# Two batches of a convolutional joint network: one batch through both convolutions first, joint tiles between the other's stages, pair sums chained in PSUM

## The chip, the cores and the metric

The kernel runs on one core of a Trainium2 chip. The metric is the device time in microseconds (us) of one execution. The engines are named as the profile names them: PE (TensorE matmul), PEld (TensorE weight load), DVE (VectorE), ACT (ScalarE), POOL (GpSimd), SP (SyncE, which issues most DMAs). PSUM is the memory that the matmuls write their sums to; the program divides it into eight banks. A stall is a stretch in which PE has nothing to run.

## The reference, cut to what matters

```python
B, T, D, K, U = 2, 4000, 512, 5, 8
def reference(x, w1, w2, g, w_f, w_g, w_o):
    h = sum over i<5 of  xp[:, i:i+T, :] @ w1[i]       # conv 1
    h = gelu(h)[:, ::2, :]                             # 2000 steps
    f = sum over i<5 of  hp[:, i:i+2000, :] @ w2[i]    # conv 2
    f = gelu(f)[:, ::2, :]                             # 1000 steps
    fe = f @ w_f ;  ge = g @ w_g
    j = tanh(fe[:, :, None, :] + ge[:, None, :, :])    # 1000 x 8 rows per batch
    return j @ w_o                                     # the joint product
```

Per batch there are two convolutions, one product "fe", and 1000 x 8 rows of the joint product. The kernel handles the joint product as 125 tiles of 128 rows, 62.5 for each batch. Each tile is four matmuls of 512 columns; the last is done in two halves, so that the profile counts 504 and not 500.

## The kernel before: the parts that matter

Both convolutions are computed with fast (Winograd-like) algorithms: sums and differences of inputs ("prepare") on DVE and ACT, sums of weights on DVE, fewer matmuls on PE. The first batch's conv 1 is done in three tiles (`Tile_`), everything else in `Triple`s with nine products per output chunk `m`.

A plan is made before the program is emitted. Every operation is recorded with what it reads and writes. A list scheduler then puts each engine's operations in order, from estimated costs. Afterwards each engine runs its list strictly in that order.

```python
def simulate(self, pred, succ, late):
    ...                                  # t, e: the engine that is free first, with something ready
        now = [i for i in cand[e] if ready[i] <= t + 0.02]
        i = min(now) if e in ("pe", "sp") else min(now, key=lambda i: (late[i], i))
    ...
```

PE takes the operation that comes first in program order among those that are ready; DVE and ACT take the most urgent by the scheduler's estimate. PSUM banks are handed out in program order, while the plan is recorded:

```python
banks = list(range(8))
def bank():                              # rotation, for fe and joint tiles
    banks.append(banks.pop(0))
    return banks[-1] * NT
```

A stage of a tile forms the pair sums with two DVE operations on two PSUM banks:

```python
def stages(self, m):                     # class Tile_
    n, lo = self.n, banks.pop(0)
    ...
    C, Dd = lo * NT, (lo + 1) * NT
    def sums():
        self.product("b2", m, C, True)
        self.product("a1", m, C, False)
        self.product("a2", m, Dd, True)
        c = cs[u % 2][0:n]
        act(c, ps.cols(C, n), ACT.Copy, scale=0.5)
        for o, f in ((C, 0.5), (Dd, -0.5)):
            stt("dve", ps.cols(o, n), ps.cols(Dd, n), f, c)
    def end0(): ...                      # a0, b1 accumulate onto C
    def end1(): ...                      # b3, a3 accumulate onto Dd, gelu
```

Prepare of conv 2 forms its differences by accumulating DMAs (issued on POOL):

```python
def prepare(self, by_dma=True):          # class Triple
    if by_dma:
        act(r32[1], z(0, 0, E), ACT.Copy, scale=-2.0)
        act(r32[2], z(2, 0, E), ACT.Copy, scale=-2.0)
        act(r32[0], z(4, -1, E), ACT.Copy, scale=-2.0)
        for i in (1, 2, 0):
            acc(r32[i], z(2 * i, 0, E))  # DMA with accumulate
    else:
        stt("dve", r32[1], z(0, 0, E), -2.0, z(2, 0, E))
        stt("dve", r32[2], z(2, 0, E), -2.0, z(4, 0, E))
        stt("dve", r32[0], z(4, -1, E), -2.0, z(0, 0, E))
    ...
```

And the order of the program is (`slot` puts the stages of one output chunk `m` into the program; the numbers after `m` in the later code say how many joint tiles follow each step): conv 1 of the first batch (three tiles), conv 1 of the second batch (`first[0]`, `first[1]`), conv 2 of the first (`trip[0]`), conv 2 of the second (`trip[1]`), then the joint tiles.

```python
for m in range(NK): slot(tiles[2], m) ...
for m in range(NK): slot(first[0], m) ...     # first[1].prepare, weight sums of conv 2 inside
for m in range(NK):
    slot(first[1], m)
    if m == 1:
        trip[0].prepare()
        load_last()
for m in range(NK): slot(trip[0], m) ...      # trip[1].prepare inside
for m in range(NK): slot(trip[1], m) ...      # ge, fe(0) inside
...
for jt in range(ntile): ...                   # 125 joint tiles; fe(1) at tile 8
```

## Time and profile before

| | before |
|---|---|
| time, median (four runs) | 270.9 us (270.75 to 271.46) |
| span in the profile | 269.3 us |
| PE / DVE / ACT busy | 261.0 / 198.2 / 181.7 us |
| PE idle between 20 and 120 us | 3.5 us |

These are lines of the profile page of the kernel before. The first two give busy time, share of the span and number of instructions of each engine. The others give the busy tenths of 40 equal slices of the span (6.7 us each), and the granted TensorE clock in tenths.

```profile
## 1 busy us (share of the span) xinstructions
PE 261.0 (97%) x1571; PEld 151.5 (56%) x1582; DVE 198.2 (74%) x288; ACT 181.7 (67%) x269; POOL 20.0 (7%) x32
...
PE   8999999999999988999999999999999999999995
...
DVE  0999999999999799697252365567666667656764
...
PEclk9999999999999999999999999999999999999999
```

PE is busy almost everywhere, at full clock. Apart from the first and the last slice, only two (94 to 108 us) fall below 9. DVE is full from about 7 to 83 us. So PE bounds the kernel, and the most that a reordering can win is PE's idle time.

The windows view gives that idle time in numbers. Its columns are the stretch and its length, then busy us and number of instructions of PE, PEld, DVE, ACT, POOL, then granted clock, DMA share and GB/s. Kernel before:

```profile
60.00:70.00 10.00, 9.51 (x63) 5.82 (x62) 10.00 (x13) 9.54 (x17) 2.92 (x3) 1.00 0.28 53
...
90.00:100.00 10.00, 8.69 (x61) 5.58 (x59) 8.01 (x14) 8.09 (x15) 1.32 (x2) 1.00 1.16 214
100.00:110.00 10.00, 9.30 (x66) 6.08 (x64) 9.93 (x13) 8.19 (x15) 2.73 (x3) 1.00 0.87 228
110.00:120.00 10.00, 9.51 (x68) 6.34 (x66) 7.86 (x12) 6.54 (x14) 1.28 (x1) 1.00 0.80 157
120.00:140.00 20.00, 20.00 (x156) 13.85 (x154) 10.71 (x18) 10.41 (x22) 0.00 (x0) 1.00 0.00 1
```

The missing parts of the ten-microsecond stretches from 20 to 120 us add up to 3.5 us (0.21 in 20 to 30, 0.49, 0.13, 0.18, 1.31, 0.70, 0.49 from 60 on). After 120 us PE has no stall worth naming.

What PE waited for in the worst stretch is in the timeline of PE, before. Its columns are start, length, engine, line, operation, output and inputs, count; in brackets, the idle time before it and what ended it.

```profile
96.45 0.74 PE L435 MATMUL acc<-zx,w_q 128*128 128x335 bf16 x4 [1.31 <-ACT sd L427]
102.59 0.74 PE L435 MATMUL acc<-hT,w_t 128*128 128x334 bf16 x4 [0.70 <-DVE hT L422]
```

### The profile page before, as it was taken

How to read it: one execution, taken by the hardware profiler on the slowest of the kernel's cores; microseconds unless marked ns; L12 is line 12 of the kernel's file. 1: busy time of each engine (PE TensorE's matmuls, PEld its weight loads, DVE VectorE, ACT ScalarE, POOL GpSimd, SP SyncE). 2: the span in 40 equal slices, each digit the busy share in tenths (PEclk: the TensorE clock that was granted, in tenths of full speed). 3: DMA queues.
4: the chain of work that ended last, by engine and by line, in shares of the span. 5: the costliest groups of instructions: out<-in, count | busy, mean ns of one | idle time of the engine just before them, and what ended most of it. 6: DMA issues, size and time to landing. Idle time of an engine off the chain costs nothing.

```text
span 269.3 us, 4218 instructions
## 1 busy us (share of the span) xinstructions
PE 261.0 (97%) x1571; PEld 151.5 (56%) x1582; DVE 198.2 (74%) x288; ACT 181.7 (67%) x269; POOL 20.0 (7%) x32
## 2 busy tenths in 40 slices
PE   8999999999999988999999999999999999999995
PEld 4897944466566645666766555444444444444442
DVE  0999999999999799697252365567666667656764
ACT  2667975459778697854489965579669769669110
POOL 1000000002533312300000000000000000000000
PEclk9999999999999999999999999999999999999999
DMA  7999999990996997940000130444544454443544
GB/s 247 306 176 223 168 177 197 197 333 4 179 215 121 212 207 234 223 87 2 0 1 2 39 117 22 153 147 136 165 161 155 133 164 149 163 155 126 170 151 142
DMA packets 61985, 40.13 MB, mean 149 GB/s; under 512 B 31742, under 2 KB 61710, under 8 KB 61966
## 3 DMA queue, kind: packets, MB, share of 16 engines
q1 hardware_dynamic: 54430, 31.49, 43.4%
q0 software_dynamic: 7392, 8.32, 16.9%
q8 instruction: 12, 0.20, 0.3%
q10 hardware_dynamic: 144, 0.07, 0.1%
q14 instruction: 7, 0.06, 0.1%
HBM read 7.86 MB, written 16.38 MB: 90 GB/s over the span
## 4 chain that ended last, share of the span: by engine, by line
PE 71%; DMA 12%; DVE 6%; issue 4%; SPq 2%; ACT 2%; POOL 2%; POOLq 0%; DVEq 0%
PE acc L435 71%; DMA r32b<-hT 6%; DMA half<-w_sb 2%; SPq L466 2%; DMA xs<-in_x_dram 2%; DMA w_sb<-in_w_dram 2%; POOL half L596 2%; DMA xr<-in_x_dram 1%; DVE hT L422 1%; DVE row L422 1%; DVE xt L422 1%; DVE row L756 1%; DVE w_t L422 1%; ACT hT L427 0%; DVE sd L422 0%
## 5 line engine op out<-in xcount | busy, mean ns | idle before, releaser
L435 PE MATMUL acc<-wo_sb,jT 128*128 128x512 bf16 (+1 forms) x493 | 107.5, 377 | 0.6
L1070 DVE CAST ost<-acc 128x512 bf16<-128x512 f32 (+1 forms) x105 | 72.2, 689 | 39.6 <-PE acc L435 39.6
L427 ACT ACTIVATE jT<-feT,geT 128x1000 bf16<-128x1000 f32 (+10 forms) x84 | 72.6, 927 | 16.9 <-PE acc L435 16.9
L435 PEld LDWEIGHTS acc<-wo_sb,jT 128*128 128x128 bf16 x504 | 49.3, 98 | 58.4
L427 ACT ACTIVATE ost<-acc 128x512 bf16<-128x512 f32 (+1 forms) x21 | 12.1, 577 | 22.5 <-PE acc L435 22.5
L435 PE MATMUL acc<-xt,w_sb 128*128 128x252 bf16 (+1 forms) x144 | 23.0, 305 | 0.2
L435 PE MATMUL acc<-row,w_sb 128*128 128x334 bf16 (+1 forms) x112 | 20.3, 305 | 0.0
L427 ACT ACTIVATE sd<-acc 128x334 f32<-128x334 f32 (+1 forms) x32 | 14.1, 447 | 8.6 <-PE acc L435 8.6
L435 PEld LDWEIGHTS acc<-xt,w_sb 128*128 128x128 bf16 x144 | 13.8, 98 | 7.5 <-DVE xt L422 1.0
L435 PE MATMUL acc<-row,w_t 128*128 128x334 bf16 (+1 forms) x80 | 14.6, 305 | 0.0
L435 PE MATMUL acc<-fT,wf_sb 128*128 128x333 bf16 (+1 forms) x96 | 14.0, 305 | 0.0
L435 PE MATMUL acc<-xs,w_t 128*128 128x252 bf16 (+1 forms) x76 | 13.9, 314 | 0.0
L427 ACT ACTIVATE hT<-acc 128x334 bf16<-128x334 f32 (+2 forms) x21 | 11.3, 552 | 3.8 <-PE acc L435 3.8
L435 PEld LDWEIGHTS acc<-row,w_sb 128*128 128x128 bf16 x112 | 10.7, 97 | 5.4 <-DVE sd L422 0.5
L422 DVE TENSOR_TENSOR sd<-sd 128x334 f32<-128x334 f32 (+1 forms) x16 | 8.0, 499 | 7.0 <-ACT sd L427 7.0
L596 POOL DMA_DIRECT2D half<-w_sb x8 | 11.8, 1489 | 18.2 <-DMA half<-w_sb 9.0
L427 ACT ACTIVATE xt<-xs 128x1008 bf16<-128x1008 bf16 (+1 forms) x8 | 10.6, 1347 | 3.0 <-DMA xs<-in_x_dram 3.0
L435 PE MATMUL acc<-hT,w_t 128*128 128x334 bf16 x64 | 11.4, 305 | 1.2 <-DVE hT L422 0.7
L435 PEld LDWEIGHTS acc<-fT,wf_sb 128*128 128x128 bf16 x96 | 9.3, 97 | 4.5
L591 DVE SCALAR_TENSOR_TENSOR acc<-acc,sd 128x334 f32<-128x334 f32 (+1 forms) x16 | 8.1, 507 | 5.0 <-PE acc L435 5.0
L435 PE MATMUL acc<-zx,w_sb 128*128 128x334 bf16 (+1 forms) x64 | 11.7, 305 | 0.0
L435 PE MATMUL acc<-hT,w_sb 128*128 128x334 bf16 x64 | 11.7, 305 | 0.0
(84 smaller groups left out, 338.3 us busy)
## 6 DMA issues: line engine op xcount, KB each, us to landing
out_dram<-ost SPq DMA_DIRECT2D x109, 128.0 KB, 1.9
w_sb<-in_w_dram SPq DMA_DIRECT2D x10, 512.0 KB, 5.5
half<-w_sb POOLq DMA_DIRECT2D x8, 512.0 KB, 5.5
r32b<-hT POOLq DMA_DIRECT2D x6, 672.0 KB, 6.9
xr<-in_x_dram SPq DMA_DIRECT2D x2, 512.0 KB, 4.2
wf_sb<-in_w_f_dram SPq DMA_DIRECT2D x1, 512.0 KB, 4.4
wg_sb<-in_w_g_dram SPq DMA_DIRECT2D x1, 512.0 KB, 5.2
wo_sb<-in_w_o_dram SPq DMA_DIRECT2D x1, 512.0 KB, 6.0
```

Of the source, the lines that this page charges most:

```text
L422: pl.op(eng, lambda e: e.tensor_tensor(out=o.ap, in0=a.ap, in1=b.ap, op=op), (a, b), (o,), vec_cost(o, (a, b)))
L427: pl.op("act", lambda e: e.activation(o.ap, i.ap, func, scale=scale, bias=0.0 if bias is None else bias.ap), rd, (o,), o.ap.free_size() * ...
L435: ins = e.matmul(o.ap, lhsT=l.ap, rhs=r.ap, start=start and n == 0, stop=stop and n == len(pairs) - 1, skip_group_check=not check)
L466: pl.dma("sp", lambda e: e.dma_start_transpose(out=dst.ap, in_=src), (), (dst,), nbytes=(hi - lo) * D * 2, rate=180e3)
L591: pl.op(eng, lambda e: e.scalar_tensor_tensor(out=o.ap, in0=a.ap, scalar=f, in1=b.ap, op0=ALU.mult, op1=add), (a, b), (o,), vec_cost(o, (a ...
L596: pl.accs.append(pl.dma("pool", lambda e: e.dma_start(dst.ap, src.ap, accum_op=add), (src, dst), (dst,), nbytes=P * 4 * dst.ap.free_size()))
L756: pl.op("dve", lambda e: e.scalar_tensor_tensor(out=o.ap, in0=a.ap, scalar=-1.0, in1=b.ap, op0=ALU.mult, op1=sub), (a, b), (o,), vec_cost( ...
L1070: pl.op("dve", lambda e, o=o, v=v: e.tensor_copy(out=o.ap, in_=v.ap), (v,), (o,), vec_cost(o, (v,)))
```

## The change

Its intent: take one batch through both convolutions and fe first, so that its joint tiles exist early and can be put between the stages of the other batch. A stage that waits then has independent PE work beside it. In addition the pair sums of a tile stage stay in one PSUM bank, which saves a DVE operation; the weights are scaled by 0.5 to fit. The rest of the diff is a new memory layout, prepare in parts of one or two input chunks, all on DVE (`by_dma=False`), and the weight sums of conv 2 moved forward. The core of it:

```diff
-                C, Dd = lo * NT, (lo + 1) * NT
-                def sums():
...
-                    self.product("a2", m, Dd, True)
-                    c = cs[u % 2][0:n]
-                    act(c, ps.cols(C, n), ACT.Copy, scale=0.5)
-                    for o, f in ((C, 0.5), (Dd, -0.5)):
-                        stt("dve", ps.cols(o, n), ps.cols(Dd, n), f, c)
+                def one():
+                    self.product("b2", m, e * NT, True)
+                    self.product("a1", m, e * NT, False)
+                    act(k, E, ACT.Copy, scale=2.0)
+                def two():
+                    self.product("a2", m, e * NT, False)
+                    f_at.append(fbanks.pop(0))
+                    tt("dve", F(), k, E, sub)
...
+        def w2quads(h):                          # weights of product t2
+            v, t = half[h][:], w2_t[1, :, sl]
+            act(v, w2_sb[4, :, sl], ACT.Copy, scale=4.0)
+            act(t, w2_sb[2, :, sl], ACT.Copy, scale=2.0)
+            acc(v, w2_sb[0, :, sl])              # DMA with accumulate
+            acc(v, t)                            # DMA with accumulate
+            act(t, v, ACT.Copy, scale=1.0 / 3.0)
...
-        for m in range(NK): slot(first[0], m) ...          # (old order, see above)
+        for h in range(2): w2quads(h)
+        for m in range(NK): w2sums(m)
+        for m in range(NK): slot(tiles[2], m) ...
+        tail_zero(0, 0, 2); trip[0].prepare(0, 2); slot()
+        tail_zero(0, 2, 3); trip[0].prepare(2, 3); slot()
+        tail_zero(0, 3, 4); trip[0].prepare(3, 4)
...
+        units = [trip[0].stages(m, 3) for m in range(NK)]  # first products need 3 of 4 chunks
...
+        ge(); w1extra(); pads(1); fe(0)
+        for lo, hi in ((0, 256), (256, 512), (512, T2)):
+            for k in range(NK): tanh(0, k, lo, hi)
+        for i in range(2):
+            first[i].prepare(0, 2); first[i].prepare(2, 4)
+            if i == 0: joint(6)
+            for m in range(NK): slot(first[i], m, (1, 0, 1, 0, 1))   # joint tiles inside
+        ...                                                # trip[1].prepare in three parts, 11 tiles
+        for m in range(NK): slot(trip[1], m, (1, 1, 1, 0, 1))
+        ...
+        fe(1); joint(ntile - state[0])
```

(The statements joined by semicolons stand on lines of their own in the source.)

## The prediction

> **What bounds the kernel now.** TensorE. In the page's first part PE is busy 261.0 of 269.3 us at a granted clock of 1.0; DVE has 74%, ACT 67%. From the timeline of TensorE I take the pitch of each width: 252 columns 0.1075 us, 498 columns 0.210, 334 columns 0.142, joint tiles of 512 columns 0.219. By the source there are 236, 112, 576 (plus 96 in the fe products) and 500 of them: 25.4 + 23.5 + 81.8 + 13.6 + 109.6 = 254 us, with transposes and ge about 257. TensorE runs from the first transpose (5.4) to 266.3, 261 us. So only about 4 us are stalls: 0.7 at 21 to 24 us, and 3.3 between 60 and 120 us in the windows view, most of them waits for an ACT copy or for DVE (1.3 at 96 us, 0.7 at 102). After 120 us there are none. The Trainium skill, "TensorE: Matmul & The Clock Gate" (section on the 2.5 ns), gives N / 2.4 GHz + 2.5 ns per warm matmul; 334 columns agree, 512 are 3 ns slower.
>
> **What the change does.** No matmul goes away. One batch goes through both convolutions and fe first (about 88 us), then its 62 joint tiles go between the other batch's stages, so that a waiting stage has independent work beside it. That saves at most those 3.3 us. The pair sums stay in one bank: one DVE op in place of two in tile stages, and one of 252 in place of two of 252 and one of 504 for the second tile, together some 6 us of DVE (0.41, 0.67 each). But DVE is full from 13 to 83 us, and the w2 sums (20 ops, about 10 us) move forward, onto DVE instead of DMA accumulates.
>
> **What it costs.** Work that hid latencies is gone in three places:
> 1. Tiles to conv 2 of the first batch. TensorE ends the tiles near 57.6 us (before's times less the triple stages between). By my count DVE ends tile work and w2 sums near 48, then has 15 us of prepare, whose last quarter waits for the last gelu (58.3). Split products (24 matmuls, 3.4 us) and the urgent parts of prepare cover most. Stall: 1 to 2 us.
> 2. Its fe to its first joint tile: copy 0.6, tanh of 256 columns 0.35, semaphores: about 1.3 us.
> 3. The other fe to its first joint tiles: two old tiles (1.75 us) against copies and four tanh of up to 1.1 us: about 1.5 us.
> The new dependence inside the second tile's stages, on a full DVE, adds perhaps 0.5. Start and tail (3 us after the last matmul) are unchanged.
>
> **Sum.** 270.9 - 3.5 (old stalls) + 4.5 (new) - 2 (new stalls filled by the scheduler, which need not keep program order) = 269.9 us. Range 267.2 to 274.6. Faster by over 2%: 0.03; within 2%: 0.87; slower by over 2%: 0.10.
>
> **What would show it.** PE busy stays 258 to 262 us with unchanged pitches; stalls sit near 58 to 62, 88 and after the second fe, none between 100 and the second fe; DVE busy falls by a few us; ACT rises slightly (more, shorter pieces); output DMA starts near 90 us.
>
> **What would make it wrong.** If DVE falls further behind before 60 us (late w2, list order), stall 1 grows to 5 to 8 us: slower. If joint tiles wait on only four output buffers or on borrowed PSUM banks, the interleaved stretch stalls. If alternating widths change TensorE's pitch, all sums move.

## More of the kernel before

The 1.31 us were a wait for an ACT copy into `sd`. The timeline of ACT just before it, same kernel, shows why that copy was late:

```profile
91.86 0.44 ACT L427 ACTIVATE sd<-acc 128x335 f32<-128x335 f32 x1
93.89 1.32 ACT L427 ACTIVATE hT<-hT 128x1336 bf16<-128x1336 bf16 x1 [1.58 <-DMA r32b<-hT]
95.11 0.43 ACT L427 ACTIVATE hT<-acc 128x334 bf16<-128x334 f32 x1
95.44 0.62 ACT L427 ACTIVATE w_t<-ws 128x512 bf16<-128x512 f32 x1
95.96 0.44 ACT L427 ACTIVATE sd<-acc 128x335 f32<-128x335 f32 x1
```

ACT stood idle for 1.58 us in front of `hT<-hT`, which waited for an accumulating DMA of prepare. Three operations later came the `sd` copy that PE needed.

## The result, and the profile after

| | before | after |
|---|---|---|
| time, median | 270.9 us (270.75 to 271.46, four runs) | 271.9 us (271.45 to 272.31, four runs) |
| ratio | | 1.0033, 95% interval 1.0009 to 1.0056 |
| span in the profile | 269.3 | 270.5 |
| PE / DVE / ACT / POOL busy | 261.0 / 198.2 / 181.7 / 20.0 | 261.2 / 199.4 / 183.1 / 7.5 |
| PE idle, 20 to 120 us | 3.5 | 4.8 |

Ratios, here and below, are the mean time of one kernel's fast runs over that of the other's of the same rounds, so they are not quite the ratio of the medians. The kernel after was not run again in the later rounds, so a comparison of an experiment with it is one of two ratios to the kernel before, from different rounds. The change is 0.33% slower. The time lies within the predicted range, 2 us above the predicted middle, and on the other side of the kernel before.

Profile page, kernel after:

```profile
PE 261.2 (97%) x1582; PEld 152.4 (56%) x1582; DVE 199.4 (74%) x352; ACT 183.1 (68%) x306; POOL 7.5 (3%) x26
...
PE   8999999979999799999999999999999999999995
...
DVE  0999999899999999993333799953424667656654
```

PE's work is the same (261.2 against 261.0 us). The weak slices have moved from 94 to 108 us to about 54 to 61 and 88 to 95 us. The windows view of the kernel after shows the idle time:

```profile
50.00:60.00 10.00, 8.30 (x40) 3.67 (x38) 8.79 (x18) 7.80 (x14) 1.15 (x3) 1.00 0.75 140
...
80.00:90.00 10.00, 8.49 (x73) 5.68 (x72) 10.00 (x19) 6.11 (x12) 0.00 (x0) 1.00 0.23 43
90.00:100.00 10.00, 8.99 (x48) 4.28 (x47) 10.00 (x17) 10.00 (x18) 0.00 (x0) 1.00 0.07 26
100.00:110.00 10.00, 10.00 (x60) 5.76 (x59) 9.67 (x19) 10.00 (x21) 0.00 (x0) 1.00 0.36 123
```

From 20 to 120 us PE lacks 0.51 (20 to 30), 1.70 (50 to 60), 0.03, 1.51 and 1.01 us (80 to 100): 4.8 us, against 3.5 before. The difference, 1.25 us, is the 1.2 us by which the span grew. All of before's stalls from 60 to 120 us are gone, and in their place stand these, from the timeline of PE, after:

```profile
60.03 0.60 PE L417 MATMUL acc<-hT,w_t 128*128 128x334 bf16 x3 [1.73 <-DVE hT L404]
...
89.53 0.74 PE L417 MATMUL acc<-zx,w_t 128*128 128x334 bf16 x4 [1.35 <-DVE feT L973]
...
91.39 3.63 PE L417 MATMUL acc<-wo_sb,jT 128*128 128x512 bf16 x16 [0.56 <-ACT jT L409]
...
99.76 1.04 PE L417 MATMUL acc<-wo_sb,jT 128*128 128x512 bf16 x4 [0.45 <-ACT jT L409]
```

The first is the passage from conv 1 to conv 2 of the first batch, the others the passage from its fe to its joint tiles. After 99.76 us PE never stops. The chain of waits of the kernel after says it in one line (start, length, what):

```profile
99.76 167.41 PE acc L417 x936
```

So the question is no longer whether PE is full behind 100 us, but why it stalls in front of it. For the first stall, the timeline of ACT, after, shows something I had not counted. `hT<-acc 128x498` are the gelus of conv 1; `w_t<-half` are the last scalings of the conv 2 weights (`w2quads`):

```profile
51.45 1.06 ACT L409 ACTIVATE w_t<-half 128x1024 bf16<-128x1024 f32 x1 [1.22 <-DMA half<-w_t]
52.41 0.57 ACT L409 ACTIVATE hT<-acc 128x498 bf16<-128x498 f32 x1
...
54.48 1.06 ACT L409 ACTIVATE w_t<-half 128x1024 bf16<-128x1024 f32 x1 [0.98 <-DMA half<-w_t]
55.44 0.57 ACT L409 ACTIVATE hT<-acc 128x498 bf16<-128x498 f32 x1
...
56.95 0.57 ACT L409 ACTIVATE hT<-acc 128x498 bf16<-128x498 f32 x1
...
58.58 0.58 ACT L409 ACTIVATE hT<-acc 128x498 bf16<-128x498 f32 x1
```

By the trace of PE the products of these four gelus ended at 50.7, 53.3, 54.9 and 56.6 us. The gelus started 1.7, 2.2, 2.0 and 2.0 us later. In front of the first two stands an operation that waited for a DMA, with ACT idle for 1.22 and 0.98 us. The wait is only about half of the delay: from the end of its product the first gelu lost 0.7 us to the wait and 1.0 us to the scaling itself, the second 1.0 us to each. The Trainium skill, "TensorE: Matmul & The Clock Gate" (section on the architecture of the array, paragraph on queue depths), says that ACT and DVE are strict first-in first-out queues. So a ready gelu cannot pass a scaling that waits. The timeline of DVE, after, shows what the late gelus delay: twice DVE stood idle before a part of the prepare, waiting for a small memset on POOL that itself follows a gelu.

```profile
53.20 2.40 DVE L585 SCALAR_TENSOR_TENSOR r32b<-hT 128x672 f32<-128x672 bf16 x3 [0.68 <-POOL hT L401]
...
57.73 1.35 DVE L585 SCALAR_TENSOR_TENSOR r32b<-hT 128x336 f32<-128x336 bf16 x3 [0.53 <-POOL hT L401]
```

That was a theory at this point; the experiments below test it.

### The profile page after: what moved, and what is told of

Its sections match the earlier page's. It is cut to its first block, busy times and chain, and to the rows that moved or that the text cites. A ratio compares the mean times of both kernels' runs of the same rounds, so it can differ in the third digit from the quotient of the medians.

```text
span 270.5 us, 4327 instructions
## 1 busy us (share of the span) xinstructions
PE 261.2 (97%) x1582; PEld 152.4 (56%) x1582; DVE 199.4 (74%) x352; ACT 183.1 (68%) x306; POOL 7.5 (3%) x26
## 4 chain that ended last, share of the span: by engine, by line
PE 69%; DVE 13%; issue 7%; ACT 5%; DMA 5%; POOL 0%; DVEq 0%; POOLq 0%
PE acc L417 68%; ACT jT L409 4%; DMA half<-w_sb 3%; DMA half<-w_t 2%; DVE row L404 2%; DVE r L585 2%; DVE hT L404 1%; DVE r32b L585 1%; DVE row L740 1%; PE acc L510 1%; DVE row L585 1%; DVE feT L973 1%; DVE xt L404 1%; DVE r L404 1%; DVE zx L404 1%
## 5 line engine op out<-in xcount | busy, mean ns | idle before, releaser
L417 PE MATMUL acc<-wo_sb,jT 128*128 128x512 bf16 (+1 forms) x504 | 115.3, 377 | 1.0 <-ACT jT L409 1.0
L1020 DVE CAST ost<-acc 128x512 bf16<-128x512 f32 (+1 forms) x95 | 65.0, 688 | 32.2 <-PE acc L417 32.1
L409 ACT ACTIVATE jT<-feT,geT 128x1000 bf16<-128x1000 f32 (+16 forms) x100 | 75.4, 816 | 8.3 <-PE acc L417 8.2
L417 PE MATMUL acc<-row,w_sb 128*128 128x334 bf16 (+1 forms) x160 | 29.8, 305 | 0.0
L417 PE MATMUL acc<-hT,w_t 128*128 128x334 bf16 x96 | 17.7, 305 | 1.7 <-DVE hT L404 1.7
L409 ACT ACTIVATE hT<-acc 128x334 bf16<-128x334 f32 (+3 forms) x33 | 15.0, 461 | 4.8 <-PE acc L417 4.6
L417 PEld LDWEIGHTS acc<-hT,w_t 128*128 128x128 bf16 x96 | 9.3, 98 | 8.1 <-DVE hT L404 2.2
L973 DVE COPY feT<-acc 128x333 f32<-128x333 f32 (+1 forms) x12 | 7.2, 616 | 8.0 <-PE acc L417 8.0
L409 ACT ACTIVATE fT<-acc 128x334 bf16<-128x334 f32 (+1 forms) x16 | 7.1, 446 | 8.6 <-PE acc L417 8.6
L417 PEld LDWEIGHTS acc<-zx,w_sb 128*128 128x128 bf16 x96 | 9.4, 98 | 5.4
```

The source lines that it names most:

```text
L409: pl.op("act", lambda e: e.activation(o.ap, i.ap, func, scale=scale, bias=0.0 if bias is None else bias.ap), rd, (o,), o.ap.free_size() * ...
L417: ins = e.matmul(o.ap, lhsT=l.ap, rhs=r.ap, start=start and n == 0, stop=stop and n == len(pairs) - 1, skip_group_check=not check)
L973: pl.op("dve", lambda e, o=o, v=v: e.tensor_copy(out=o.ap, in_=v.ap), (v,), (o,), vec_cost(o, (v,)))
L1020: pl.op("dve", lambda e, o=o, v=v: e.tensor_copy(out=o.ap, in_=v.ap), (v,), (o,), vec_cost(o, (v,)))
```

## The experiments

Two theories of the stalls were put against each other. The queue theory: the stalls come from what stands in front of urgent work, in the order of an engine or in the order in which PSUM banks are given out. The load theory, that of my prediction: DVE (and ACT) simply have too much to do around the passages. And for what the interleaving buys: everywhere between the stages, or only at one place.

### e1_nofill: no joint tiles between the stages

```diff
-            if i == 0: joint(6)
-            for m in range(NK): slot(first[i], m, (1, 0, 1, 0, 1))
+            for m in range(NK): slot(first[i], m)
...
-        slot(None, 0, (0, 1, 1, 0, 1))      # twice, between the parts of trip[1].prepare
+        slot()
...
-        joint(6)
-        for m in range(NK): slot(trip[1], m, (1, 1, 1, 0, 1))
+        for m in range(NK): slot(trip[1], m)
```

(The output buffers are those that the later tiles use; the four early ones are not needed.)

> Edit: the changed kernel, but all joint tiles come after the second fe; none between the other batch's stages. Theory A (interleaving itself removed the old stalls): without it TensorE stalls come back between 90 and 170 us, 2 to 4 us in all, and the time is 273 to 276 us. Rival B (the old stalls came from the prepare of conv 2 by accumulating DMA, which the changed kernel no longer uses there): between 100 us and the second fe no stall over 0.5 us in all, only the first wait near 88 us may grow because no joint tile covers the prepare of the next triple; 271 to 273.5 us. DVE and ACT busy the same within 2 us under both.

Measured: 278.97 us median, ratio to before 1.0296 (1.0261 to 1.0330). Timeline of PE and windows view of e1_nofill:

```profile
136.75 2.38 PE L417 MATMUL acc<-hT,w_t 128*128 128x334 bf16 x8 [6.18 <-issue]
```

```profile
130.00:137.00 7.00, 0.82 (x6) 0.33 (x5) 7.00 (x18) 1.35 (x3) 0.12 (x1) 0.74 0.00 0
137.00:139.00 2.00, 2.00 (x9) 1.11 (x8) 2.00 (x8) 0.00 (x0) 0.00 (x0) 0.50 0.00 0
```

Neither theory had it right. There is one stall of 6.18 us, at the passage from conv 1 to conv 2 of the second batch, while DVE is full with prepare (7.00 of 7.00 us busy). Between the stages only 0.47 and 0.40 us of stalls show. The stall also costs clock: from 137 to 139 us the granted clock is 0.50. In the main this agrees with the Trainium skill, "TensorE: Matmul & The Clock Gate" (Part 1), which says that the clock falls to half after an idle window of about 3.4 us. Here the granted clock was 0.50 from 133.3 to 140.1 us, beginning 2.75 us after the last matmul had ended, so somewhat sooner than that figure; the stalls of the kernel after, up to 1.73 us, left it at 1.00.

So the interleaving is worth 2.6% inside the new order, but mostly because the new order itself makes a passage that nothing else covers. The order before put another batch's stages there.

### e5_transfill: joint tiles at that passage alone

```diff
-            if i == 0: joint(6)
-            for m in range(NK): slot(first[i], m, (1, 0, 1, 0, 1))
+            for m in range(NK): slot(first[i], m)
...                                          # the 11 tiles around trip[1].prepare stay
-        for m in range(NK): slot(trip[1], m, (1, 1, 1, 0, 1))
+        for m in range(NK): slot(trip[1], m)
```

> Edit: the changed kernel with only twelve joint tiles between the other batch's stages, all of them at the passage from its conv 1 to its conv 2 (where e1 showed a stall of 6.2 us); the other tiles come after the second fe. Theory A (interleaving pays at that passage alone; between the stages themselves e1 showed only 0.9 us of stalls): the 6.2 us stall goes, the granted clock stays at 1.0, 12 tiles last 10.5 us and cover it; the time is within 1 us of the changed kernel, 271 to 273 us. Rival B (the tiles between stages matter too, as the change's words suggest): stalls of 2 us or more return between 90 and 130 us and the time is 273.5 to 276 us.

Measured: 270.90 us median, ratio 1.0012 (0.9981 to 1.0043), against 1.0033 for the whole change. Timeline of PE, e5_transfill:

```profile
60.12 0.60 PE L417 MATMUL acc<-hT,w_t 128*128 128x334 bf16 x3 [1.79 <-DVE hT L404]
...
91.36 0.74 PE L417 MATMUL acc<-zx,w_b 128*128 128x334 bf16 x4 [0.83 <-ACT sd L409]
```

After 91.4 us no wait shows. Eleven tiles at one passage do what 57 tiles spread over 110 us do. (I wrote twelve before the run; the trace of e5_transfill has 44 weight loads of joint tiles before the second fe, four for each tile, and that of the kernel after has 228, between 91.4 and 200.1 us.) The intervals overlap, so I don't call it faster than the change; but the tiles between stages are not what fills PE. The Trainium skill, "Perfetto Trace Analysis" (section Optimization Strategy), says that interleaving regimes with different contended engines may improve performance. This agrees for the passage, where DVE was full and PE idle, and not for the stages, where PE was the full engine already.

### e2_unchain: pair sums without the chain

```diff
-                    act(k, E, ACT.Copy, scale=2.0)
+                    act(k, E, ACT.Copy)
...
-                    self.product("a2", m, e * NT, False)
                     f_at.append(fbanks.pop(0))
-                    tt("dve", F(), k, E, sub)
+                    self.product("a2", m, f_at[0] * NT, True)
+                    tt("dve", E, k, F(), add)
+                    tt("dve", F(), k, F(), sub)
```

> Edit: the changed kernel with the pair sums of the tile stages undone: a2 goes to its own PSUM bank and two DVE ops form sum and difference, as before. Adds one DVE op to eight stages (4 of 252 columns at 0.42 us, 4 of 498 at 0.68), 4.4 us of DVE before 52 us. If DVE before 60 us is what sets the stall at 58 us (the step of the prediction), the stall grows by 2 to 4 us and the time to 273.5 to 276. If the stall is set by the chain over ACT (late gelus) and DVE has slack there, the stall grows by less than 1 us: 271.5 to 273 us.

Measured: 272.38 us median, ratio 1.0056 (1.0028 to 1.0085). Timeline of PE, e2_unchain:

```profile
59.99 0.60 PE L417 MATMUL acc<-hT,w_t 128*128 128x334 bf16 x3 [2.05 <-DVE hT L404]
```

Undoing the chain moves the stall at 58 us by 0.3 us (1.73 to 2.05), and the time by about 0.6 us (1.0056 less 1.0033, times 271), which the intervals don't separate from nothing. The load theory expected 2 to 4 us. But the test was weaker than planned. DVE's busy time grew by 3.3 us in all (199.4 to 202.7) and not by 4.4, and by only 1.7 us before 53.15 us (45.39 to 47.11), in part because the scheduler moved three sums of conv 2 weights to a later place. Prepare began at 53.14 us, against 53.20 before the edit: so DVE's load in front of the passage did not set its start. That load has no share at all in the stall is not shown by this run.

### e4_quadlate: the late scalings behind the gelus

```diff
             acc(v, t)
-            act(t, v, ACT.Copy, scale=1.0 / 3.0)
...
         slot()
+        gel = pl.ops[-1].idx                  # the last gelu of conv 1
         tail_zero(0, 3, 4)
         trip[0].prepare(3, 4)
+        for h in range(2):
+            t = w2_t[1, :, 2 * h * P:2 * (h + 1) * P]
+            act(t, half[h][:], ACT.Copy, scale=1.0 / 3.0)
+            pl.ops[-1].after.append(gel)      # not before that gelu
```

> Edit: the two ACT scalings that wait for the accumulating DMAs of the w2 quads may run only after the last gelu of conv 1. Theory A (ACT runs in order; the two scalings wait for DMA at 51.4 and 54.5 us and hold up the gelus behind them by 1.3 to 2.1 us, which starts the prepare late): gelus start within 0.5 us of their last product, the stall at 58 us falls from 1.73 us to below 0.4, time 1.3 to 1.8 us lower than the changed kernel. Rival B, as predicted (the amount of DVE work sets it): prepare ends no earlier, stall stays 1.4 to 1.9 us, time within 0.4 us. Miss to watch: the third product stage then waits for the later scaling near 67 us.

Measured: 270.21 us median, ratio 0.9972 (0.9950 to 0.9994). Timelines of ACT and of PE, e4_quadlate:

```profile
50.51 0.59 ACT L409 ACTIVATE hT<-acc 128x498 bf16<-128x498 f32 x1
...
53.03 0.59 ACT L409 ACTIVATE hT<-acc 128x498 bf16<-128x498 f32 x1 [0.38 <-PE acc L417]
...
55.25 0.57 ACT L409 ACTIVATE hT<-acc 128x498 bf16<-128x498 f32 x1
56.39 0.59 ACT L409 ACTIVATE hT<-acc 128x498 bf16<-128x498 f32 x1 [0.57 <-PE acc L417]
...
58.84 2.00 ACT L409 ACTIVATE w_t<-half 128x1024 bf16<-128x1024 f32 x2
```

```profile
58.78 0.60 PE L417 MATMUL acc<-hT,w_t 128*128 128x334 bf16 x3 [0.75 <-DVE hT L404]
```

The same four gelus now start at 50.51, 53.03, 55.25 and 56.39 us, against 52.41, 55.44, 56.95 and 58.58: two of them directly upon the product they wait for, as the brackets show. The stall fell from 1.73 to 0.75 us, less far than I wrote (below 0.4). The time fell by 0.61% of before (1.0033 to 0.9972, intervals that do not overlap), about 1.65 us, as expected by the queue theory. No DVE or ACT work was taken away, but the two scalings, 2.00 us of ACT, now run behind the gelus. So the run shows that what stood in front of the gelus cost the time; it does not separate the wait for the DMA from the scalings' own length. The 0.75 us that is left looks different: DVE is busy for all of the 6.85 us from 53.15 to 60 us, against 6.27 us in the kernel after, so for this rest the count of DVE work may be right. The wait that I feared near 67 us did not come.

An earlier attempt at the same end, moving other scalings to a later place in the program, was built but not run: the list scheduler gave the same order on ACT, since it goes by its own estimate of urgency and not by program order. (This is not shown.)

### e3_slotfirst: the next stage unit gets its bank before the joint tiles

```diff
             if i == 0:
+                slot(first[0], 0)
                 joint(6)
-            for m in range(NK):
+            for m in range(1 - i, NK):
                 slot(first[i], m, (1, 0, 1, 0, 1))
```

> Edit: the first stage unit of the other batch's conv 1 is put before the six joint tiles in program order, so that it gets its PSUM bank from an older fe product. Theory A (the 1.35 us wait at 88 us is for a bank whose fe copy comes last on DVE, and the 0.56 and 0.45 us after it are tanh): TensorE starts the unit at 88.2 us without waiting, the stalls between 88 and 100 us fall from 2.4 us to 0.5 to 1.2, time 1.2 to 1.9 us lower than the changed kernel. Rival B (DVE and ACT are simply full here, and what is not waited for at 88 is waited for a little later): the stalls stay 2 to 2.4 us, time within 0.5 us.

Measured: 270.62 us median, ratio 0.9989 (0.9956 to 1.0022). Timeline of PE, e3_slotfirst:

```profile
88.66 0.74 PE L417 MATMUL acc<-zx,w_t 128*128 128x334 bf16 x4 [0.52 <-ACT feT L409]
...
90.12 0.74 PE L417 MATMUL acc<-zx,w_b 128*128 128x334 bf16 x4 [0.15 <-ACT sd L409]
...
98.90 1.90 PE L417 MATMUL acc<-wo_sb,jT 128*128 128x512 bf16 x8 [0.29 <-ACT jT L409]
```

The stalls of this passage fell from 2.4 us (1.35, 0.56, 0.45) to 1.0 us, and the time by 0.44% of before, about 1.2 us. By time alone this gain is not clear of the noise, since the interval overlaps that of the kernel after (1.0009 to 1.0056); the stalls carry the reading. The stall at 58 us was also shorter in this run, 1.44 us against 1.73. In the kernel after, the first unit of the second batch was recorded behind six joint tiles. It therefore got the bank of one of the last fe products, whose copy on DVE ended at 89.47 us (started at 88.84, 0.63 us long); PE started at 89.53. Recorded first, it takes an older bank. The scheduler could have reordered the matmuls, but not the bank that was already given out.

### c1_both, c2_split, c3_hold: the repairs together

c1_both has the edits of e3 and e4. c2_split adds this (the first products of conv 2 start with two chunks instead of three):

```diff
-                    self.product("s1", m, e, True, range(split))
-                    self.product("t1", m, e, False, range(split))
+                    self.product("s1", m, e, True, range(split - 1))
+                    self.product("t1", m, e, False, range(split - 1))
+                def mid():                       # run for all m before the stages
+                    self.product("s1", m, e, False, range(split - 1, split))
+                    self.product("t1", m, e, False, range(split - 1, split))
```

and c3_hold adds this to c2_split:

```diff
+        kept = banks.pop(0)
         fe(0)
+        banks.insert(0, kept)
```

> Both edits of e3 and e4 at once (late w2 scalings on ACT, first stage unit before the six joint tiles). If the two stalls are independent, their gains add: 0.9972 and 0.9989 against before, the changed kernel 1.0033, so 0.993 of before, about 269.0 us; stalls left: 0.5 at 24 us, 0.75 at 58, 1.0 between 88 and 100. If they share a cause (DVE full from 40 to 110 us), the gain is no more than that of the better one: 270.2 us.

> c1, and the split products of conv 2 start with two input chunks instead of three, so that TensorE has 16 matmuls (2.3 us) that need only the first prepare. If the rest of the stall at 58 us is the wait for the second prepare, it goes from 0.75 to below 0.2 us and the time is 0.5 us lower than c1 (268.5). If the third prepare then ends too late (it ended at 61.3 us in e4, work lasts to 61.5), a new wait of about 0.5 us shows near 61 us and nothing is gained.

> c2, and one PSUM bank is kept out of the second fe rotation for the first stage unit. If the 0.52 us wait at 88 us in e3 is for the bank of one of the last fe copies, it goes to 0 and the time is 0.3 to 0.5 us lower than c2; fe with seven banks must not stall itself. If it is for operands of prepare, nothing changes.

| run | median us | ratio to before | 95% interval |
|---|---|---|---|
| c1_both | 269.34 | 0.9932 | 0.9911 to 0.9952 |
| c2_split | 269.25 | 0.9935 | 0.9912 to 0.9958 |
| c3_hold | 269.11 | 0.9925 | 0.9905 to 0.9946 |

The two gains add: 0.9932, where the sum of the separate ones said 0.993, as closely as intervals of 0.2% can tell. That speaks against a common cause. In c1_both PE still waits 0.31 us at 58 us (0.75 expected) and 0.49 and 0.21 us between 88 and 100. These are all the waits of PE over 0.15 us in c3_hold, from its timeline:

```profile
1.19 4.23 PE L417 MATMUL acc<-zero 128*128 128x512 bf16 x10 [1.19 <-DVE zero L424]
24.13 0.60 PE L417 MATMUL acc<-xs,w_t 128*128 128x252 bf16 x4 [1.11 <-DVE ty L404]
79.64 7.00 PE L417 MATMUL acc<-fT,wf_sb 128*128 128x333 bf16 x48 [0.63 <-ACT fT L409]
98.20 1.90 PE L417 MATMUL acc<-wo_sb,jT 128*128 128x512 bf16 x8 [0.51 <-ACT jT L409]
```

The stalls at 58 and at 88 us are gone. But both are gone in c2_split already, where no wait over 0.15 us shows between 26 and 80 us nor between 81 and 99 us: the split does what it was made for, and of the kept bank no effect is shown. The 0.5 us that I expected of the split in time, and the 0.3 to 0.5 us of the kept bank, did not come: c2_split and c3_hold are not faster than c1_both by more than the intervals allow. Other small waits have grown meanwhile: at 24 us from 0.5 us in the kernel after to 1.1, before fe from 0.16 to 0.63. An edit at one place changes the scheduler's estimates and so the order elsewhere. Whether the second half of the gain was lost to that was not tried.

All three beat both kernels, by 0.7% against before (for c3_hold at least 0.5% by the interval).

### b1_dveprep: the same idea in the kernel before

One word, in the kernel before:

```diff
-                trip[0].prepare()
+                trip[0].prepare(False)
```

> The kernel before with one word changed: the prepare of its first conv 2 forms its three differences on DVE (3 ops of 1.55 us) instead of by accumulating DMAs of 6.9 us. If before's stalls at 83 to 103 us came from engines in order behind an instruction that waits for those DMAs (ACT and DVE both idle 1.6 and 2.0 us until 93.9 us), the 1.3 and 0.7 us stalls fall below 0.7 us in sum and the time is 1 to 1.5 us below before (ratio 0.995). If DVE, which is 80 to 93 per cent busy there, is the limit, the stalls stay or grow, ratio 0.999 to 1.005.

Measured: 269.63 us median, ratio 0.9938 (0.9918 to 0.9957). Windows view and timeline of PE, b1_dveprep:

```profile
90.00:100.00 10.00, 10.00 (x72) 6.85 (x71) 10.00 (x14) 7.02 (x14) 0.00 (x0) 1.00 0.67 177
100.00:110.00 10.00, 10.00 (x72) 6.68 (x71) 10.00 (x16) 7.36 (x13) 1.28 (x2) 1.00 0.07 24
```

```profile
60.56 0.74 PE L435 MATMUL acc<-zx,w_t 128*128 128x334 bf16 x4 [1.83 <-ACT hT L427]
```

From 90 to 120 us PE is now full, where before it lacked 2.5 us, although DVE got three operations of 1.55 us more and is itself full there. So before's largest stalls did come from the differences by accumulating DMA. The same word also takes the three scalings in front of those DMAs off ACT (about 1.3 us each), so the run does not separate the wait for the DMAs from that load; the idle waits for `r32b<-hT` in the trace of the kernel before, 1.58 us on ACT and 1.99 us on DVE, speak for the wait. The edit also shifted the order around 58 us, where a new wait of 1.83 us appeared. In sum the profile shows about 0.8 us less from the first convolution matmul to the last matmul. The medians differ by 1.65 us; about 0.4 us of that is an earlier start in the profiled run (7.45 against 7.84 us), which varies from run to run, and the rest I can't place.

One word in the kernel before thus reached what the rewritten kernel reached only after repair.

## Why the prediction was right or wrong

**Right: what bounds the kernel.** PE work stayed (261.2 against 261.0 us busy), and the change moved only idle time. The time lies in the range and within 2% of before, as given 0.87. The range was wide enough for either sign, though, and the sign was missed: I forecast 1 us less and it became 1 us more.

**Right in the main: the old stalls go.** I counted 3.3 us from 60 to 120 us; in the kernel after, none of these waits is left. That the joint tiles between the stages were the reason was wrong: e5_transfill has none of them between the stages and no wait there after 91.4 us, and b1_dveprep removes the stalls of 90 to 120 us in the old order by taking the accumulating DMAs out.

**Stall 1, conv 1 to conv 2: size right, cause wrong.** I gave 1 to 2 us; it measured 1.73. The step was a count of DVE work ("DVE ends tile work and w2 sums near 48, then has 15 us of prepare"). e2_unchain put 3.3 us of DVE back, 1.7 us of it before the passage, and moved it by 0.3 us; e4_quadlate took no work away, changed only the order on ACT, and brought it to 0.75 us. What is left may be DVE work. What failed is the assumption that the gelus run when their products end; they ran about 2 us later, behind two scalings that waited for a DMA and were 1.06 us long themselves.

**Stall 2, fe to first joint tile: 1.3 predicted, 2.4 measured (1.35 + 0.56 + 0.45).** The mechanism I named, copy and tanh, is the smaller part. The 1.35 us were a wait for a PSUM bank given out behind six joint tiles (e3_slotfirst), and the 0.45 us come from ACT, which is full from 90 to 100 us with the first two thousand columns of tanh.

**Stall 3, second fe to its joint tiles: 1.5 predicted, none measured.** I counted two old tiles left to cover it. The kernel after has run 57 tiles before the second fe (the last unbroken run of joint matmuls starts at 208.3 us and ends at 267.2; at 0.2155 us each that is 68 of 125 tiles), so some five and a half tiles of the first batch, 4.7 us, were left. The overlap that I had too small was this count of old tiles: two in the prediction, about five and a half in the run.

**The step of the sum that failed.** I credited 2 us for "new stalls filled by the scheduler, which need not keep program order". No such filling shows. When the plan is made, PE's list may pass over a matmul that is not ready, but it can't pass over a bank that the program gave to another, and ACT and DVE can't pass over anything once their order is fixed. Without that credit the sum would have been 271.9 us, which is the measured median; but since stalls 2 and 3 missed in opposite directions, part of that agreement is chance.

**DVE busy: wrong.** I expected a fall of a few us; it rose from 198.2 to 199.4. I had seen that the sums of the conv 2 weights came onto DVE, but not that prepare of conv 2 came onto DVE too: six operations of 1.55 us when whole. POOL, which issued those DMAs, fell from 20.0 to 7.5 us.

**A misread pitch.** I took 0.219 us for a matmul of 512 columns from the kernel before, and wrote that it is slower than N / 2.4 GHz + 2.5 ns. The page of before counts 493 matmuls of the joint product where 504 weights were loaded, so some records are missing and the pitch was too long: nine of the steps from one record to the next are 0.43 us, twice the others. In the kernel after all 504 are there, and four of them take 0.862 us when alternating with other stages (185.20 to 186.06): 0.2155 us each. That agrees with the Trainium skill, "TensorE: Matmul & The Clock Gate" (section on the 2.5 ns): 512 / 2.4 GHz + 2.5 ns is 0.2158 us. Alternating widths cost nothing.

ACT rose slightly (181.7 to 183.1), and the first output DMA was issued at 93.5 us, both near what I wrote.

## What to carry to other kernels

When the bound engine stalls for a copy by another engine, look at what stands in front of that copy in its in-order queue. An operation there that waits for a DMA delays everything behind it by the wait and by its own length, and one dependence that holds it back until after the urgent work can be worth more than a new order of the whole program. Interleaving independent work pays at the passages where one engine must finish before another can go on, not between stages where the bound engine is full already; and buffers given out in program order can undo what a scheduler gains by reordering.

## What the Trainium skill lacked or had wrong

- "TensorE: Matmul & The Clock Gate" says that ACT and DVE queues are strict first-in first-out, but neither it nor "Perfetto Trace Analysis" (Identifying Dependency Chains) says what follows when a queued operation waits for a DMA: here two scalings on ACT with such waits of 1.22 and 0.98 us, and 1.06 us long themselves, made ready gelus start about 2 us late, and moving them was worth about 1.65 us of 272.
- "DMA: Bandwidth & Descriptors" says that a DMA with accumulate must be issued from GpSimd, and gives no time for an accumulating one, only a general fit of time by size, by which an estimate for 512 KB is 3.2 us. Here one of 512 KB took 5.1 to 6.4 us from issue to landing, one of 672 KB 6.9 us (medians), and the same 672 KB difference took DVE 1.55 us.
- "Perfetto Trace Analysis" (Optimization Strategy) recommends interleaving regimes, without a word on where. Here 11 joint tiles at one passage (ratio to before 1.0012) did as much as 57 spread over all stages (1.0033).
- "Perfetto Trace Analysis" (Matmuls) advises rotating through banks so that evacuation overlaps, but doesn't warn that a bank given out in program order ties a matmul to the copy that last used it: 1.35 us here, 0.52 after one unit was moved.
- "Perfetto Trace Analysis" (Matmuls) does not warn that a trace can lack matmul records: 493 of 504 joint matmuls in the kernel before, 504 of 504 in the kernel after, which turned a pitch of 0.2155 us into one of 0.219.
